# Norm weights folded into the weight conversion, row scaling on ScalarE, 48-row loads and a new order for the first 420 steps of a recurrent-attention and two-layer feed-forward kernel

## The chip, the cores and the metric

The kernel runs on one core of a Trainium2 chip. The metric is the device time of one execution in microseconds (us); it was 443.83 us before (median of 3 runs, 443.22 to 448.07).

## The reference

The input is a gated linear attention over 2 batches, 8 heads, 768 positions and head size 40, followed by two feed-forward layers on the 1536 rows of 320 features that it gives.

```
attention, for every t:  m_new = max(f + m, i)
    C = exp(f+m-m_new) * C + exp(i-m_new) * v k^T      n likewise with k
    y = sigmoid(o_gate) * (C q) / max(|n q|, 1)
layer 1:  rms = sqrt(mean(x*x) + 1e-06);  xn = x / rms * rms_g
    out1 = (silu(xn @ w_gate) * (xn @ w_val)) @ w_out      320 -> 1536 -> 320
layer 2:  h = out1 @ w_in;  max(0.01*h, h) @ w_out         320 -> 2048 -> 320
```

The weights and the output are float64 and float32 in memory: the kernel converts each weight tile from 64-bit numbers itself. `rms_g` has one number for each of the 320 features.

## The kernel before, in words

The 768 positions are cut into 6 chunks of 128, so there are 12 attention tiles T (chunk T // 2 of batch T % 2). In the early part of the program each tile passes through the same steps, and four kinds of work are interleaved by hand:

- **Gates.** DVE runs the scans over the gate rows (`sf`, `sa`), PE turns the rows into columns (`co`), ACT takes exponentials. For tiles 0 and 1, PE builds the argument of the exponential itself (`fa`, `rows_a`, from the split rows `A_hl` that `ah` writes); later tiles read it back from memory (`Ab`).
- **Attention of a tile.** PE: scores `qk` (`s`, L343). ACT: four exponentials per half (`arg`, L359). DVE: scores times exponentials (`p`, L390). PE: times the values (`av`, L403), the state of earlier chunks (`inn`, L413) and the new state (`kv`, L425). DVE: output gate `y1` (L458), reciprocal, `yr` (L472). ACT: sum of squares `sq` (L478).
- **The norm.** `y2` in three parts: DVE makes mean + epsilon from the sum (L485), POOL raises it to -1/2 (`pow`, L487), DVE refines that with one Newton step of three instructions (L489 to L491). Then `xn` (L496, DVE) multiplies the 128 x 320 rows by that column and by `gb`, the norm weights spread over all partitions; `xc` (ACT) copies 64 columns, `tp` (L507, PE) transposes, `xh` (ACT) and `xl` (L515, DVE) split the result into a high and a low part of `X`.
- **Weight conversion.** Each tile of A (512 columns), R (256) and B (320) weights goes through a shift on DVE (L548), a Prelu on ACT (L550), a shift-or on DVE (L552), a rounded copy on ACT (L573, L616, L627) and the remainder on DVE (L575, L619, L630).

The first feed-forward products, `U` (L658), need `X` of three tiles: `U.0.*` those of tiles 0 to 2, `U.1.*` those of tiles 3 to 5. `D` (L730) multiplies by the B weights. Each engine takes its instructions strictly in the order of the list `ORDER`, whose tokens name a step and its indices; there is no other scheduler. The token `id.1` is a product of ones (L229, `busy`) whose result nobody reads. The queue SP issues all transfers, in the same order list; q and k come by `ld_qk` (two halves of 40 rows of 4 KB, into one of three buffers), and `e` rows by `ld_e` (two halves of 40 rows of 2 KB).

Of the kernel before, what the change touches and what calls it, by code (L numbers as in the profile page):

```python
# [18 lines left out]
L = 128  # L19
# [36 lines left out]
wR.2 r.2 mask.3.1 rec.0 wA.1 a.1 rec.1 r.2 dq.2 a.1 yr.0 id.1 mask.3.0 arg.3.0 r.2 id.1 r.2 qk.2 th.1 st.0 y1.1 de.2
dA.2.6 eq.2 ux.1.2 co.1.1.2 cv.1.1.2 cv.0.2.6 sq.0 y2.0.0 yr.1 wA.2 kv.1 dgb p.2.0 av.2.0 arg.2.1 y2.0.1 p.2.1 y2.0.2
k.2 sq.1 y2.1.0 a.2 y2.1.1 a.1 xn.0 a.2 arg.3.1 a.1 dq.3 qk.3 p.3.1 dq.4 cb.0 wB.1 a.2 xc.0 b.1 dsl y2.1.2 th.2 a.2
dr.2.6 da.4 mask.4.1 wA.4 xn.1 av.2.1 inn.2 y1.2 xc.1 id.1 st.1 abs.2 id.1 id.1 id.1 p.3.0 rec.2 tp.0 id.1 b.1 tp.1
dn.3 yr.2 dr.1.2 mask.4.0 dc.1.2 a.4 sq.2 b.1 y2.2.0 kv.2 xh.1 wR.3 th.3 de.3 dE.2.6 k.3 b.1 id.1 xh.0 xl.0 av.3.0  # L60
co.1.2.6 cv.1.2.6 xl.1 cb.1 y2.2.1 y2.2.2 r.3 qk.4 eq.3 av.3.1 inn.3 dv.1.2 xn.2 arg.4.0 xc.2 tp.2 abs.3 r.3 r.3 c.3
rec.3 dn.5 kv.3 a.4 xh.2 arg.4.1 xl.2 U.0.1.1 p.4.0 k.5 y1.3 da.5 a.4 st.3 U.0.1.0 cb.3 p.4.1 th.5 T.0.1 dn.4 th.4
mask.5.0 wA.3 yr.3 sq.3 a.4 E.0.1 mask.5.1 a.3 arg.5.1 dc.2.6 de.4 r.3 arg.5.0 y2.3.0 a.3 eq.4 M.0.1 av.4.0 av.4.1
inn.4 dq.5 qk.5 y2.3.1 y1.4 p.5.1 U.0.0.0 p.5.0 T.0.0 E.0.0 dv.2.6 U.0.0.1 M.0.0 da.6 mask.6.1 arg.6.1 de.5 wB.0 abs.4
dq.6 a.3 rec.4 mask.6.0 av.5.0 av.5.1 S.0.1 eq.5 y2.3.2 yr.4 S.0.0 inn.5 kv.5 abs.5 b.0 xn.3 rec.5 b.0 sq.4 y2.4.0
# [103 lines left out]
def body(ctx: ExitStack, tc, ig, fg, qk, nat, wgv, wgr, wo1, wi2, wi2r, wo2, rg, cst, cst2, out):  # L169
# [940 lines left out]
```

## Time and profile before

| | |
|---|---|
| median of 3 runs | 443.83 us (443.22 to 448.07) |
| profiled execution, its own time | 444.82 us |
| span of the profiled execution | 443.0 us |
| PE busy | 429.1 us, 97% |
| DVE busy | 367.9 us, 83% |
| ACT busy | 280.7 us, 63% |
| POOL busy | 104.5 us, 24% |
| chain that ended last | PE 83%, DVE 8%, ACT 4%, DMA 2%, issue 2% |

PE is TensorE's product unit, DVE VectorE, ACT ScalarE, POOL GpSimd, SP the queue that issues transfers. Busy shares over the whole span hide that the program has stages: the first 80 us hold the attention of eight tiles and the conversion of the first weights, and the rest is nearly all feed-forward. So the profile is read by stretches, and for each stretch one asks what PE waited for and at which clock it ran.

### The profile page before, as it was taken

The numbers are of one execution on the slowest core, as the hardware profiler recorded it, in microseconds if no ns is written. First come the engines' busy times: TensorE is split into PE (matmuls) and PEld (weight loads), VectorE is DVE, ScalarE is ACT, GpSimd is POOL, SyncE is SP. The second block draws the span as 40 slices with busy tenths as digits, with TensorE's granted clock in tenths as the row PEclk, the third lists the DMA queues.
The fourth block names the chain that finished last, engine by engine and source line by source line (L and its number), as shares of the span: only waits on it lengthen the run. The fifth ranks groups of instructions, "written<-read, shape, count | busy, mean of one in ns | idle before, by whom it ended". The sixth has DMA issues, their size and how long they took to land.

```text
span 443.0 us, 9728 instructions
## 1 busy us (share of the span) xinstructions
PE 429.1 (97%) x3702; PEld 409.6 (92%) x3704; DVE 367.9 (83%) x827; ACT 280.7 (63%) x708; POOL 104.5 (24%) x166
## 2 busy tenths in 40 slices
PE   8897989999999999999999999999999999999997
PEld 4775978999999989999999999999999999999996
DVE  7998999677787758969989999888679897988775
ACT  5777866674664377644565565987866676577442
POOL 4644462431212000463736210010101010110000
PEclk9559999999999999999999999999999999999999
DMA  7987593653602124121200000004012311101005
GB/s 220 320 304 248 181 323 115 222 169 115 223 2 78 56 77 123 57 84 39 85 2 2 1 0 1 1 9 148 30 34 74 108 48 32 30 31 31 0 2 178
DMA packets 16119, 42.14 MB, mean 95 GB/s; under 512 B 2056, under 2 KB 4040, under 8 KB 16072
## 3 DMA queue, kind: packets, MB, share of 16 engines
q1 hardware_dynamic: 16072, 41.52, 28.4%
q8 instruction: 29, 0.48, 0.4%
q14 instruction: 18, 0.15, 0.1%
HBM read 39.45 MB, written 2.06 MB: 94 GB/s over the span
## 4 chain that ended last, share of the span: by engine, by line
PE 83%; DVE 8%; ACT 4%; DMA 2%; issue 2%; SPq 0%; DVEq 0%; ACTq 0%
PE h L808 13%; PE xa L730 10%; PE v L658 8%; PE g L658 8%; PE oa L981 6%; PE oa L979 6%; PE oa L980 6%; PE u L808 6%; PE xw L748 5%; PE h L814 3%; PE h L813 3%; PE s L343 2%; PE o L403 2%; PE u L813 1%; DMA Ab<-A_d 1%
## 5 line engine op out<-in xcount | busy, mean ns | idle before, releaser
L981 PE MATMUL oa<-wB,xl 128*128 128x320 f32 x192 | 59.3, 309 | 0.0
L980 PE MATMUL oa<-wB,xh 128*128 128x320 f32 x192 | 59.3, 309 | 0.0
L979 PE MATMUL oa<-wB,xh 128*128 128x320 f32 x192 | 59.3, 309 | 0.0
L658 PE MATMUL g<-X,wA 128*128 128x384 f32 x256 | 50.3, 341 | 1.8 <-DVE th L690 0.9
L991 DVE TENSOR_TENSOR x<-oa,x 128x320 f32<-128x320 f32 x84 | 39.5, 484 | 14.6 <-PE oa L981 13.9
L658 PE MATMUL v<-X,wA 128*128 128x384 f32 x256 | 49.9, 339 | 0.9 <-ACT X L511 0.7
L658 PEld LDWEIGHTS g<-X,wA 128*128 128x128 f32 x256 | 44.2, 188 | 3.9 <-DVE th L690 1.2
L658 PEld LDWEIGHTS v<-X,wA 128*128 128x128 f32 x256 | 44.5, 188 | 1.5 <-ACT X L511 0.8
L730 PE MATMUL xa<-sh,wB 128*128 128x384 f32 x160 | 45.9, 337 | 0.0
L590 POOL TENSOR_TENSOR sums<-w_A 128x128 f32<-128x128 f32 x8 | 3.9, 487 | 151.6 <-DVE w_A L552 147.0
L981 PEld LDWEIGHTS oa<-wB,xl 128*128 128x128 f32 x192 | 36.1, 188 | 0.1
L980 PEld LDWEIGHTS oa<-wB,xh 128*128 128x128 f32 x192 | 36.0, 188 | 0.0
L979 PEld LDWEIGHTS oa<-wB,xh 128*128 128x128 f32 x192 | 36.0, 188 | 0.0
L808 PE MATMUL h<-X,wA 128*128 128x384 f32 x144 | 32.2, 338 | 0.0
L730 PE MATMUL xa<-sl,wB 128*128 128x384 f32 x96 | 32.2, 336 | 0.0
L955 ACT ACTIVATE c<-c 128x384 f32<-128x384 f32 x48 | 25.2, 524 | 7.2 <-DVE c L852 3.4
L730 PEld LDWEIGHTS xa<-sh,wB 128*128 128x128 f32 x160 | 29.4, 188 | 0.1
L965 DVE TENSOR_TENSOR xl<-c,xh 128x384 fp32r<-128x384 f32 x48 | 26.0, 556 | 1.0 <-ACT xh L960 0.8
L960 ACT CAST xh<-c 128x384 fp32r<-128x384 f32 x48 | 24.3, 513 | 2.9 <-PE oa L980 2.2
L359 ACT ACTIVATE w<-Ab,aeu 128x128 f32<-128x128 f32 x80 | 25.3, 392 | 0.6 <-POOL Ab L363 0.6
L808 PEld LDWEIGHTS h<-X,wA 128*128 128x128 f32 x144 | 25.0, 188 | 0.1
L487 POOL TENSOR_TENSOR sm<-sm,mhalf 128x1 f32<-128x1 f32 x12 | 7.9, 661 | 66.5 <-DVE sm L485 66.5
(204 smaller groups left out, 1124.8 us busy)
## 6 DMA issues: line engine op xcount, KB each, us to landing
raw_B<-wo SPq DMA_DIRECT2D x28, 320.0 KB
raw_A<-wgv SPq DMA_DIRECT2D x12, 512.0 KB
nat<-nat SPq DMA_DIRECT2D x12, 484.0 KB
Ab<-A_d SPq DMA_DIRECT2D x10, 512.0 KB
raw_A<-wi SPq DMA_DIRECT2D x8, 512.0 KB
qkt<-qk SPq DMA_DIRECT2D x24, 160.0 KB
out<-x SPq DMA_DIRECT2D x12, 160.0 KB
eb<-e_d SPq DMA_DIRECT2D x20, 80.0 KB
```

The lines of the kernel that those rows point to most:

```text
L359: A.activation(w[:, j], src, AF.Exp, scale=-1.0, bias=col)
L658: PE.matmul(dst, a, x, start=(i == 0), stop=(i == len(seq) - 1))
L730: PE.matmul(xa, w, x, start=(k == 0), stop=(k == len(seq) - 1))
L748: PE.matmul(xas["w", g, i], a, x, start=(f == NE and k == 0), stop=(f == NF - 1 and k == len(seq) - 1),)
L808: PE.matmul(dst, x, y, start=first and j == 0, stop=j == 2, skip_group_check=not first)
L955: A.activation(t, src, AF.Prelu, alpha=0.01)
L960: A.copy(v["h"], v["t"])
L965: V.tensor_tensor(v["l"], v["t"], v["h"].bitcast(F32), op=ALU.subtract)
L979: PE.matmul(oa, v["h"][:, ts], wb[:, 0:DM], start=m == 0, stop=False)
L980: PE.matmul(oa, v["h"][:, ts], wb[:, DM:], start=False, stop=False)
L981: PE.matmul(oa, v["l"][:, ts], wb[:, 0:DM], start=False, stop=m == 1)
L991: V.tensor_tensor(dst, oas[k, p, i], dst, op=ALU.add)
```

## The change

It has five parts.

1. The norm weights are loaded as three columns `gcol` (128 x 3) in place of `gb` (128 x 320 by broadcast), and multiplied into the A and R weights of layer 1 when these are converted. ACT's copy of 512 columns becomes two scaled copies of 256, and DVE's remainder two instructions of 256 with a multiplication and a subtraction.
2. `xn`, now a scaling of the rows by one column alone, goes from DVE to ACT.
3. Epsilon is a 321st column of `y`, set once; the square on ACT carries the scale, so the sum comes out as the mean, and DVE's `y2.T.0` (L485) goes. The Newton step takes two instructions instead of three (the sign sits in the reciprocal's factor).
4. q, k and `e` are loaded as 48 rows per half instead of 40; the added rows are not used by the products.
5. The first 420 of some 1,930 tokens of the order are new. After `K.0.0.1`, `U.1.2.1` begins a tail that is the same as before but for the `y2.T.0` tokens. The number of `id.1` is 24 in both.

```diff
-id.1 id.1 id.1 id.1 z.0 z.1 z.2 did cr id.1 id.1 dfg dig id.1 id.1 id.1 wR.1 dq.0 ms id.1 sf.0.1 sa.0.1 ah sf.1.2 id.1
+ms id.1 z.4 id.1 dig cl z.5 z.0 z.2 z.1 dfg sf.0.1 sa.0.1 sf.1.2 sa.1.2 ev.1.2 did cr co.0.1.2 cv.0.1.2 uv.0.1 ah.0
...
-        for r in (slice(0, D), slice(64, 64 + D)):
+        for r in (slice(0, 48), slice(64, 112)):
             Q.dma_start(out=qkt[r].rearrange("p a j t -> p (a j t)"), in_=qk[T, r])
...
-            Q.dma_start(out=eb[64 * e:64 * e + D].rearrange("p j l -> p (j l)"), in_=e_v[b, c, e].partition_broadcast(D))
+            Q.dma_start(out=eb[64 * e:64 * e + 48].rearrange("p j l -> p (j l)"), in_=e_v[b, c, e].partition_broadcast(48))
...
-        A.activation(junk, t["yf"], AF.Square, accum_out=t["sm"][:, 8:9])
+        A.activation(junk, t["yx"], AF.Square, scale=2.0 * DM ** -0.5, accum_out=t["sm"][:, 8:9])
...
-        if i == 0:
-            V.tensor_scalar(out=v_, in0=ss, scalar1=1.0 / DM, scalar2=1e-6, op0=ALU.mult, op1=ALU.add)
-        elif i == 1:
+        if i == 1:
             G.tensor_tensor(z, v_, mhalf, op=ALU.pow)
         else:
             V.tensor_scalar(out=z2, in0=z, scalar1=z, scalar2=v_, op0=ALU.mult, op1=ALU.mult)
-            V.tensor_scalar(out=z2, in0=z2, scalar1=-0.5, scalar2=1.5, op0=ALU.mult, op1=ALU.add)
-            V.tensor_tensor(z, z, z2, op=ALU.mult)
+            V.tensor_scalar(out=zn, in0=z2, scalar1=3.0, scalar2=z, op0=ALU.subtract, op1=ALU.mult)
...
-        V.scalar_tensor_tensor(out=xn[:, 0:DM], in0=t["yf"], scalar=t["z"], in1=gb, op0=ALU.mult, op1=ALU.mult)
+        A.activation(xn[:, 0:DM], t["yf"], AF.Copy, scale=t["z"])
...
-        A.copy(w[:, 0:2], x)
+        for k in range(2):
+            A.activation(w[:, k], x[:, k], AF.Copy, scale=gcol[:, k:k + 1])
         yield
-        V.tensor_tensor(w[:, 2:4], x, w[:, 0:2].bitcast(F32), op=ALU.subtract)
+        for k in range(2):
+            V.scalar_tensor_tensor(
+                out=w[:, 2 + k], in0=x[:, k], scalar=gcol[:, k:k + 1], in1=w[:, k].bitcast(F32), op0=ALU.mult, op1=ALU.subtract,
+            )
```

What the new order moves is seen in the engines' own lists. First PE's list at the start of the program, before, from the ninth product of ones to the first scores (`pt` are columns, `A` the arguments of `fa`, `s0` the scores of tile 0):

```order
L229 MATMUL busy_138<-const-bfloat16-1.0 128x512
L229 MATMUL busy_150<-const-bfloat16-1.0 128x512
L229 MATMUL busy_159<-const-bfloat16-1.0 128x512
L251 MATMUL pt0_0_165<-consts_87,x2_92 128x16
L261 MATMUL A0_0_178<-consts_r_88 128x512
L264 MATMUL A0_0_178<-A_hl_89,consts_r_88 128x128 x4
L261 MATMUL A1_1_191<-consts_r_88 128x512
L264 MATMUL A1_1_191<-A_hl_89,consts_r_88 128x128 x4
L261 MATMUL A0_1_203<-consts_r_88 128x512
L264 MATMUL A0_1_203<-A_hl_89,consts_r_88 128x128 x4
```

And the same place now, from PE's first product:

```order
L230 MATMUL busy_127<-const-bfloat16-1.0 128x512
L230 MATMUL busy_130<-const-bfloat16-1.0 128x512
L252 MATMUL pt0_1_153<-consts_87,x2_92 128x16
L252 MATMUL pt0_0_167<-consts_87,x2_92 128x16
L262 MATMUL A1_0_175<-consts_r_88 128x512
L265 MATMUL A1_0_175<-A_hl_89,consts_r_88 128x128 x4
L262 MATMUL A1_1_198<-consts_r_88 128x512
L265 MATMUL A1_1_198<-A_hl_89,consts_r_88 128x128 x4
L252 MATMUL pt1_0_204<-consts_87,x2_92 128x16
L262 MATMUL A0_0_218<-consts_r_88 128x512
```

Eleven products of ones at the front became two, and the arguments of tile 1 come ahead of those of tile 0.

Second, PE's list around the state product of tile 2 (`o1_2` from `Cbd0`), before:

```order
L403 MATMUL o1_2_494<-nat2_238,w2_1_511 32x41 x16
L413 MATMUL o1_2_494<-Cbd0_98,eb2_105 32x82 x16
L229 MATMUL busy_615<-const-bfloat16-1.0 128x512
L229 MATMUL busy_620<-const-bfloat16-1.0 128x512
L229 MATMUL busy_622<-const-bfloat16-1.0 128x512
L229 MATMUL busy_624<-const-bfloat16-1.0 128x512
L507 MATMUL tp0_629<-consts_87,xn0_531 128x128 x3
```

And now, from the last of tile 1's state products to the state product of tile 2:

```order
L426 MATMUL o1_1_383<-nat1_172,Kt1_110 40x41
L230 MATMUL busy_538<-const-bfloat16-1.0 128x512
L230 MATMUL busy_545<-const-bfloat16-1.0 128x512
L230 MATMUL busy_547<-const-bfloat16-1.0 128x512
L230 MATMUL busy_569<-const-bfloat16-1.0 128x512
L230 MATMUL busy_571<-const-bfloat16-1.0 128x512
L252 MATMUL pt1_1_573<-consts_87,x2_92 128x16
L230 MATMUL busy_579<-const-bfloat16-1.0 128x512
L230 MATMUL busy_581<-const-bfloat16-1.0 128x512
L414 MATMUL o1_2_450<-Cbd0_98,eb2_105 32x82 x16
```

Seven products of ones now stand right ahead of that state product (three more follow it), where four followed it before.

Third, DVE's list from the remainder of the B weights of tile 2's time to `X` of tile 2 (`sm2` are the norm's columns of tile 2, `X` from `tp0`, `tp1`, `tp2` the split of tiles 0, 1, 2), before:

```order
L631 TENSOR_TENSOR wB_1_654<-w32_B1_561,wB_1_654 128x64
L515 TENSOR_TENSOR X_93<-tp0_629,X_93 128x3x128
L255 COPY aeu_94<-pt1_2_698 128x64
L515 TENSOR_TENSOR X_93<-tp1_636,X_93 128x3x128
L489 TENSOR_SCALAR sm2_618<-sm2_618 128x1
L490 TENSOR_SCALAR sm2_618<-sm2_618 128x1
L491 TENSOR_TENSOR sm2_618<-sm2_618 128x1
L548 TENSOR_SCALAR w32_R3_711<-raw_R3_667 128x256
L305 COPY gdec_95<-pg1_647 128x8
L496 SCALAR_TENSOR_TENSOR xn2_758<-y2_612,sm2_618,gb_91 128x320
```

And now:

```order
L578 SCALAR_TENSOR_TENSOR wA_2_475<-w32_A2_492,gcol_91,wA_2_475 128x256 x2
L489 TENSOR_SCALAR sm2_599<-sm2_599 128x1
L490 TENSOR_SCALAR sm2_599<-sm2_599 128x1
L306 COPY gdec_95<-pg1_682 128x8
L553 SCALAR_TENSOR_TENSOR w32_A4_694<-raw_A4_684,w32_A4_694 128x512
L514 TENSOR_TENSOR X_93<-tp0_671,X_93 128x3x128
L256 COPY aeu_94<-pt0_2_713 128x64
L460 SCALAR_TENSOR_TENSOR y0_106<-nat3_543,o1_3_618 128x320
L514 TENSOR_TENSOR X_93<-tp1_707,X_93 128x3x128
L514 TENSOR_TENSOR X_93<-tp2_760,X_93 128x3x128
```

The norm's columns of tile 2 have moved ahead of `X` of tiles 0 and 1, `xn2` has left DVE's list, and the three `X` splits stand close together.

## Rows read from the trace of the kernel before

**Rows 1.** Busy time by stretch: us; PE, PEld, DVE, ACT, POOL (instructions), granted clock, DMA share, GB/s

```profile
0.00:10.65 10.65, 8.62 (x32) 4.25 (x32) 8.32 (x21) 5.94 (x17) 5.04 (x18) 1.00 0.76 221
10.65:34.50 23.85, 21.26 (x337) 16.45 (x337) 22.29 (x55) 16.99 (x51) 12.69 (x18) 0.51 0.91 312
34.50:44.02 9.52, 7.06 (x163) 5.44 (x163) 7.75 (x27) 7.43 (x25) 4.45 (x8) 0.98 0.68 239
44.02:80.25 36.23, 33.84 (x606) 31.01 (x608) 33.38 (x81) 25.44 (x78) 18.31 (x27) 1.00 0.64 213
80.25:443.00 362.75, 358.35 (x2567) 352.50 (x2566) 296.15 (x646) 224.89 (x540) 64.02 (x98) 1.00 0.19 62
```

**Rows 2.** PE's waits, 0 to 80.25: us in total, times, longest

```profile
PE tp L507 <- DVE X L515: 1.3, 1, 1.3
...
PE g L658 <- DVE th L690: 0.9, 1, 0.9
```

**Rows 3.** Timeline of PE: start us, us, engine, line, operation, names, shape, count, idle before

```profile
10.45 0.50 PE L261 MATMUL A<-consts_r 128*128 128x512 f32 x1
...
11.73 4.08 PE L343 MATMUL s<-qkt 40*128 40x128 f32 x31
...
28.36 2.49 PE L343 MATMUL s<-qkt 40*128 40x128 f32 x16
...
31.33 1.32 PE L413 MATMUL o<-Cbd,eb 104*32 104x82 f32 x32
32.98 1.49 PE L229 MATMUL busy<-const-bfloat16-1.0 128*128 128x512 bf16 x3 [0.33 <-issue]
...
80.25 2.95 PE L658 MATMUL v<-X,wA 128*128 128x384 f32 x16
```

**Rows 4.** Timeline of DVE

```profile
5.03 0.28 DVE L270 TENSOR_TENSOR A_hl<-x,A_hl 16x128 fp32r<-16x128 f32 x1
...
6.17 0.47 DVE L241 TENSOR_TENSOR_SCAN x<-x 16x128 f32<-16x128 f32 x1
...
16.33 2.48 DVE L390 TENSOR_TENSOR w<-s,w 128x512 f32<-128x512 f32 x4
...
34.31 0.47 DVE L458 SCALAR_TENSOR_TENSOR y<-nat,o 128x320 f32<-128x320 f32 x1
...
40.02 0.27 DVE L489 TENSOR_SCALAR sm<-sm 128x1 f32<-128x1 f32 x1
...
62.87 2.00 DVE L496 SCALAR_TENSOR_TENSOR xn<-y,sm,gb 128x320 f32<-128x320 f32 x1
```

**Rows 5.** Timeline of POOL

```profile
37.63 0.55 POOL L487 TENSOR_TENSOR sm<-sm,mhalf 128x1 f32<-128x1 f32 x1 [1.95 <-DVE sm L485]
...
63.24 1.28 POOL L367 TENSOR_TENSOR eb<-eb,qkt 104x512 f32<-104x512 f32 x1
```

**Rows 6.** Groups of PE by form, 10.65 to 34.50: count | busy us, mean ns | idle before

```profile
L403 PE MATMUL o<-nat,w 128*32 128x41 f32 x192 | 4.2, 272 | 2.2 <-DVE w L390 1.7 <-PE o L425 0.5
...
L425 PE MATMUL o<-nat,Kt 128*64 128x41 f32 x16 | 2.2, 311 | 0.0
```

**Rows 7.** Groups of DVE by form, 0 to 80.25

```profile
L496 DVE SCALAR_TENSOR_TENSOR xn<-y,sm,gb 128x320 f32<-128x320 f32 x6 | 4.7, 783 | 0.0
...
L575 DVE TENSOR_TENSOR wA<-w_A,wA 128x512 fp32r<-128x512 f32 x5 | 3.9, 772 | 0.0
...
L485 DVE TENSOR_SCALAR sm<-sm 128x1 f32<-128x1 f32 x6 | 0.9, 148 | 0.3 <-ACT junk L478 0.3
```

**Rows 8.** Groups of ACT by form, 0 to 80.25

```profile
L359 ACT ACTIVATE w<-A,aeu 128x128 f32<-128x128 f32 x16 | 4.3, 362 | 0.5 <-DVE aeu L255 0.5
...
L447 ACT ACTIVATE nat<-nat 128x320 f32<-128x320 f32 x8 | 3.7, 464 | 0.3 <-DMA nat<-nat 0.3
...
L573 ACT CAST wA<-w_A 128x512 fp32r<-128x512 f32 x5 | 3.0, 605 | 0.0
```

**Rows 9.** A stretch in which SP issues only loads of q and k (columns of rows 1)

```profile
50.00:51.00 1.00, 1.00 (x8) 1.00 (x7) 1.00 (x4) 1.00 (x4) 1.00 (x3) 1.00 0.65 246
```

More of the change, by code (lines that the diff above doesn't have):

```diff
@@ L56 @@
[L56 to L65, printed above, removed]
@@ L193, in body @@
     consts_r = attc.tile([128, 272], F32R, name="consts_r")
-    A_hl = attc.tile([48, L], F32R, name="A_hl")
+    A_hl = attc.tile([48, 2, L], F32R, name="A_hl")
     ident, mask = consts[:, 0:128], consts[:, 128:256]
@@ L198, in body @@
     blk = sel[:, 128:136]
-    gb = attc.tile([128, DM], F32, name="gb")
+    gcol = const.tile([128, 3], F32, name="gcol")
     x2 = const.tile([128, NTILE, 3, L], F32, name="x2")
@@ L207, in body @@
     QK = [attc.tile([128, 2, 4, L], F32, name=f"qkt{n}") for n in range(3)]
-    EB = [attc.tile([104, 4, L], F32, name=f"eb{n}") for n in range(3)]
+    EB = [attc.tile([128, 4, L], F32, name=f"eb{n}") for n in range(3)]
+    Y = [attc.tile([128, DM + 1], F32, name=f"y{n}") for n in range(3)]
     Kt = [attc.tile([128, 4, 104], F32, name=f"Kt{b}") for b in range(2)]
@@ L456, in att_y1 @@
         num = t["num"]
-        t["y"] = y = work.tile([128, H, D], F32, tag="y", name=f"y{T}")
+        t["yx"] = Y[T % 3]
+        t["y"] = y = Y[T % 3][:, 0:DM].rearrange("p (h d) -> p h d", h=H)
         V.scalar_tensor_tensor(
@@ L465, in att_rec @@
         r = t["sm"][:, 0:8]
-        V.tensor_scalar(out=r, in0=r, scalar1=1.0, scalar2=2.0, op0=ALU.max, op1=ALU.mult)
+        V.tensor_scalar(out=r, in0=r, scalar1=1.0, scalar2=-2.0, op0=ALU.max, op1=ALU.mult)
         V.reciprocal(r, r)
@@ L476, in att_sq @@
         t = st_[T]
-        junk = work.tile([128, DM], F32, tag="junk", name=f"junk{T}", bufs=1)
-        A.activation(junk, t["yf"], AF.Square, accum_out=t["sm"][:, 8:9])
+        junk = work.tile([128, DM + 1], F32, tag="junk", name=f"junk{T}", bufs=1)
+        A.activation(junk, t["yx"], AF.Square, scale=2.0 * DM ** -0.5, accum_out=t["sm"][:, 8:9])
     def att_y2(T, i):
         t = st_[T]
-        ss, v_, z, z2 = (t["sm"][:, i:i + 1] for i in range(8, 12))
-        t["z"] = z
-        if i == 0:
-            V.tensor_scalar(out=v_, in0=ss, scalar1=1.0 / DM, scalar2=1e-6, op0=ALU.mult, op1=ALU.add)
-        elif i == 1:
+        v_, z, z2, zn = (t["sm"][:, i:i + 1] for i in range(8, 12))
+        t["z"] = zn
+        if i == 1:
             G.tensor_tensor(z, v_, mhalf, op=ALU.pow)
@@ L518, in memsets @@
         G.memset(mhalf, -0.5)
+        for y in Y:
+            G.memset(y[:, DM:], (DM * 1e-6) ** 0.5)
         G.memset(A_hl.bitcast(F32), 0.0)
@@ L614, in weight_r @@
         halves = [(up_weights(2 * i + e), slice(64 * e, 64 * e + 64), slice(64 - 64 * e, 128 - 64 * e)) for e in range(2)]
+        first = i < NF // 2
         for w, hi, lo in halves:
-            A.copy(w[hi, 4], x[hi])
+            if first:
+                A.activation(w[hi, 4], x[hi], AF.Copy, scale=gcol[hi, 2:3])
+            else:
+                A.copy(w[hi, 4], x[hi])
         yield
         for w, hi, lo in halves:
-            V.tensor_tensor(w[lo, 4], x[hi], w[hi, 4].bitcast(F32), op=ALU.subtract)
+            if first:
+                V.scalar_tensor_tensor(
+                    out=w[lo, 4], in0=x[hi], scalar=gcol[hi, 2:3], in1=w[hi, 4].bitcast(F32), op0=ALU.mult, op1=ALU.subtract,
+                )
+            else:
+                V.tensor_tensor(w[lo, 4], x[hi], w[hi, 4].bitcast(F32), op=ALU.subtract)
         yield
```

232 lines of the change are left out of this document (121 added, 111 removed).

## The prediction, made before the result was known

> **What bounds the kernel now.** I read the busy time by stretch first [rows 1]. The reader is to see two programs in one. From 80.25 us on, PE is busy 358.35 of 362.75 us at a granted clock of 1.00, while DVE has 296.15 and ACT 224.89. From `U.1.2.1`, the product that starts there [rows 3], the order is the old one. So a gain or loss at that start reaches the end one for one, and the question is when 80.25 comes. Ahead of it PE is idle 2.03 us up to 10.65, 2.59 up to 34.50, 2.46 up to 44.02 and 2.39 up to 80.25, together 9.5. The second stretch stands out: at a clock of 0.51, the level of 1.2 GHz, PE's work there costs about twice what it costs at 2.4 GHz, DVE is busy 22.29 of 23.85 us, and the DMA share is 0.91.
>
> Then I read PE's waits [rows 2]: the two long ones are 1.3 us of `tp` for DVE's `X` and 0.9 of `g` for `th`. Last the timelines [rows 3 to 5], for the chain that makes the first `U` possible: scores, `p`, values, state product, `y1`, norm, `xn`, `tp`, `X`. I cut it into three terms: T1 up to `y1` of tile 2 (34.31 [rows 4]), T2 from there to `U.0.1` (44.02 [rows 1]), T3 from there to `U.1.2.1`. A gain is counted positive.
>
> **T1, the start.** PE's work is the same; only places differ. Before, `A_hl` is written by 5.31 and a second pair of scans follows until 6.64 [rows 4]. In the new order that pair (1.33 us) and some six small operations of about 0.15 each (the L485 row [rows 7]) stand ahead of `ah`: `A_hl` comes at about 7.5. With two products of ones at the front I let PE run at half clock from there. Four arguments follow, each 1.28 us (from 10.45 to 11.73 [rows 3]), until about 12.7; scores of tile 0, half of the 4.08 us that two tiles took, to 14.7. ACT's exponentials cost 4.3/16 = 0.27 us [rows 8], four of them 1.1, partly under the scores: first `p` at about 15.2, against 16.33 [rows 4], and the values of tile 0 from about 15.9.
>
> From there PE's list at half clock: values 4.2/3 = 1.4 us a tile [rows 6], scores 2.04, state 1.1 (2.2 for two [rows 6]), a product of ones 0.5 (1.49 for three [rows 3]). Up to the scores of tile 3 it is 1.4 + 2.04 + 0.5 + 2.04 + 0.7 + 0.5 + 1.1 + 0.7 + 0.5 + 0.7 = 10.2, so these start at 26.1; before it was 28.36. Scores, two products of ones, values and state (2.04 + 1.0 + 0.7 + 1.1) lead to 30.9. Then stand the seven products of ones and the state product of tile 2, which took 1.32 [rows 3]: its end lies at 33.3 at the earliest (0.23 each, half the price above, and 0.8) and 35.7 at the latest, against 32.65. DVE has to wait about 2 us for the scores of tile 1 at half clock (14.7 + 1.4 + 0.5 + 2.04 = 18.6, with its own work done by 16.6), and by the 16 us of work that its list then holds it comes to `y1` of tile 2 at about 35.0, where before it was 34.31. So T1 = **-0.7**, from +1.0 (the state product ends at 33.3 and DVE is free) to -2.7 (the dearest products, and DVE behind them by 1.3).
>
> The loads grow by a fifth (48 rows for 40) in a stretch whose DMA share is 0.91. While only such loads were in flight the share was 0.65 [rows 9], that is some 10 of the 16 engines. No row shows 48 rows. The bounds: nothing, if the rows spread over engines now idle, or a fifth of a transfer on the path, within T1's lower end; I take nothing. The Trainium skill, page "DMA: Bandwidth & Descriptors", section "Why a DMA increments its semaphore by 16 and not by 1", says that the outer size decides how many engines share a transfer, the largest divisor up to 16: 10 for 40 rows, which the 0.65 bears out, and 16 for 48. By it each engine would move 3 rows for 4, and the term would be slightly above nothing.
>
> **T2, norm and first U.** Between `y1` of tile 2 and `U.0.1` lie 9.7 us. POOL's power ended at 38.18 [rows 5], but DVE came to the Newton step at 40.02 [rows 4], since the `X` splits of tiles 0 and 1 stood ahead and waited: 1.84 us. These stand behind it now. L485 (0.15 and 0.3 of idle [rows 7]) goes, and one Newton instruction of the same kind with its hop, 0.2. That is 2.5 us at most on the norm. `xn` moves from DVE (a mean of 0.78 with its stalls [rows 7]) to ACT; the nearest row is 0.46 [rows 8]: nothing gained or lost, and ACT, busy 7.43 of 9.52 [rows 1], has room. If another ACT instruction stood ahead, the cost is up to 0.6 (the copy of 512 [rows 8]). What is late next: `X` of tiles 0 and 1, which now stand behind, and PE's own 7.06 us of work in this stretch. I take **+2.4**, from 0.8 (the splits become the last wait) to 3.4 (with all of the 0.9 us by which PE's idle time of 2.46 could shrink beyond my sum).
>
> **T3, up to U.1.2.1.** The 1.3 us stall of `tp` [rows 2] followed an `xn` that took 2.00 us, from 62.87 to 64.87, while POOL's product ran from 63.24 to 64.52 [rows 4, 5]. With `xn` on ACT this goes. The 0.9 for `th` stays. DVE, busy 33.38 of 36.23 us [rows 1], loses 4.7 us of `xn` in the first 80 us and 0.9 of L485 [rows 7]; the remainder in two pieces of 256 columns costs about the same 0.77 plus one more start of some 0.15 for each of five tiles. ACT's two scaled copies for one of 0.605 [rows 8] are bounded by 0.6 and 1.2, five times 0.3 on average, and six `xn` at 0.46 add 2.8: with 25.44 of 36.23 us ACT covers it. If that cover were gone the exponentials would be late by up to 0.6. I take **+1.2**, from -0.8 (a caught remainder takes xn's place) to 2.4 (all of PE's idle time).
>
> A rule of the Trainium skill, page "SBUF — State Buffer", section "Who interferes with whom", speaks against the change. A DVE instruction with two inputs in SBUF and a GpSimd instruction that reads SBUF exclude each other, and the first holds the other up for its whole length. The 2.00 us beside POOL's 1.28 agrees. By it each split remainder can be caught twice where it could be caught once, up to 1.28 us each time, and T3 would be -0.8 where the row of `xn` alone gives 1.2.
>
> **The sum** is -0.7 + 2.4 + 1.2 = 2.9 us. The profiled execution took 444.82, so 441.9 for it; it lay 0.99 above the median of 443.83, and the same gain from the median gives **440.9**. The ends: -2.7 + 0.8 - 0.8 = -2.7, or 446.5; and 1.0 + 3.4 + 2.4 = 6.8, or 437.0.
>
> **The rivals.** *Full gain.* All terms at their upper ends: the first scores come early enough that the norm is ready whenever PE is. For it: 9.5 us of PE's time are idle, and the order is free to fill it. Against it: DVE at 93% in two stretches. 437.0; chance 0.30.
>
> *The clock stays low (slower).* Before, the clock was 1.00 up to 10.65, fell after the products of ones at the front, and came back at 34.50, behind three of them in a row [rows 1, 3]. With two at the front it may never be 1.00 early, and if the ten around the state product of tile 2 are broken by waits for DVE, it stays at 0.5 until the `U` products. Then T1 is -2.5, and PE's work between that state product and `U.0.1`, about 7.7 us (7.06 in the stretch and what precedes 34.50 of it), takes 15.4 where 11.4 us lay before: -4.0. With T3 of 1.2 the loss is 5.3, or 449.1. It decides once more than about 40% of that work runs at half clock. Against it: ten such products nearly together are more than the three that were enough. Chance 0.08.
>
> *The change does not do what it says.* The second inputs on DVE stay (remainders, splits), POOL catches them as before, and the wider loads lengthen a DMA stage at 0.91. T1 -2.5, T2 1.0, T3 0: -1.5, or 445.3. For it: DVE's list gets shorter by only 36 of 829 instructions. Against it: the waits that go have names and places. Chance 0.17.
>
> The forecast itself, with a range of 439.4 to 443, has 0.45.
>
> **How the numbers follow.** About 1%, 4.4 us, is what a measurement of this kernel can tell from no change: 439.4 and 448.3. Faster by more takes the full gain, 0.30; slower by more takes the low clock, 0.08; the forecast and the third rival lie between, 0.62. The range leaves out the low clock and about half of the third rival on one side and the last part of the full gain on the other, some 0.2: 436.5 to 444.5.
>
> **What the next profile would show.** T1 is right if `y1` of tile 2 starts near 35 and the clock is 1.00 from about 34; wrong if the first `p` comes after 17. T2 is right if the Newton step starts within 0.3 us of POOL's end and `U.0.1` stands near 42.3; wrong if `X` of tile 0 or 1 ends the wait there. T3 is right if no wait of `tp` for `X` over 1 us is left and `U.1.2.1` starts near 77.3. The whole is wrong if the stretch behind `U.1.2.1` no longer takes 362.75 us, for instance because ACT's new work or a caught remainder stalls PE there.

## The result, and the profile after

The changed kernel took 450.65 us in the median of 10 runs (449.22 to 453.38), against 443.98 before. The ratio is 1.0126, with a 95% interval of 1.0098 to 1.0154: it is slower. Forecast were 440.9 us and a range of 436.5 to 444.5.

The profiled execution took 449.22 us, 4.40 more than that of before, so it shows two thirds of the loss of the medians (it is the fastest of the ten). First the busy time by stretch of the changed kernel (columns as in [rows 1]), cut where the three terms of the prediction end:

```profile
0.00:10.65 10.65, 5.88 (x17) 3.38 (x17) 8.58 (x26) 5.01 (x12) 4.60 (x19) 1.00 0.78 253
10.65:24.30 13.65, 12.01 (x170) 10.13 (x171) 8.60 (x19) 10.59 (x34) 5.22 (x9) 1.00 1.02 267
24.30:31.00 6.70, 3.62 (x120) 2.66 (x117) 5.73 (x16) 5.31 (x16) 3.93 (x7) 1.00 0.93 323
31.00:46.11 15.11, 13.72 (x230) 8.83 (x232) 10.71 (x33) 11.03 (x34) 8.24 (x14) 0.89 0.80 242
46.11:82.86 36.75, 34.22 (x605) 31.19 (x606) 30.48 (x77) 30.42 (x92) 17.16 (x26) 1.00 0.79 230
82.86:447.40 364.54, 358.87 (x2570) 352.61 (x2566) 293.76 (x635) 228.18 (x548) 64.79 (x98) 1.00 0.20 62
```

`U.1.2.1` starts at 82.86, where it was 80.25 [rows 3], and the stretch behind it takes 364.54, where it was 362.75 [rows 1]. So 2.61 us are lost ahead of it and 1.79 behind. DVE is no longer full: 8.60 of 13.65 us from 10.65 to 24.30, and 30.48 of 36.75 in the second stage, where it was 33.38 of 36.23. ACT has 30.42 there, where it had 25.44 [rows 1].

PE's timeline after (columns as in [rows 3]), the places of the prediction's first two terms:

```profile
13.12 2.17 PE L344 MATMUL s<-qkt 40*128 40x128 f32 x16
...
26.94 1.27 PE L344 MATMUL s<-qkt 40*128 40x128 f32 x16
...
31.61 1.04 PE L426 MATMUL o<-nat,Kt 128*64 128x41 f32 x16 [2.43 <-ACT Cbd L443]
32.59 2.31 PE L230 MATMUL busy<-const-bfloat16-1.0 128*128 128x512 bf16 x5
...
35.53 0.78 PE L414 MATMUL o<-Cbd,eb 104*32 104x82 f32 x32
...
37.78 0.66 PE L426 MATMUL o<-nat,Kt 128*64 128x41 f32 x16
...
45.52 0.44 PE L672 MATMUL g<-X,wA 128*128 128x384 f32 x1
46.11 1.49 PE L672 MATMUL g<-X,wA 128*128 128x384 f32 x7 [0.15 <-DVE X L514]
```

The same 16 scores take 2.17 us at 13.12 and 1.27 at 26.94, so PE ran at the level of 1.2 GHz until about 24 us, although the clock column stands at 1.00 there: the price tells it. Then PE waits 2.43 us for the state product of tile 1, and five products of ones behind it cost 0.46 each, the price of the low level again (the clock of that stretch is 0.89).

DVE's timeline after:

```profile
6.45 0.28 DVE L271 TENSOR_TENSOR A_hl<-x,A_hl 16x128 fp32r<-16x128 f32 x1
...
15.72 1.29 DVE L391 TENSOR_TENSOR w<-s,w 128x512 f32<-128x512 f32 x2 [1.62 <-ACT w L360]
18.46 0.49 DVE L460 SCALAR_TENSOR_TENSOR y<-nat,o 128x320 f32<-128x320 f32 x1 [1.45 <-ACT nat L448]
...
31.00 0.47 DVE L460 SCALAR_TENSOR_TENSOR y<-nat,o 128x320 f32<-128x320 f32 x1
...
38.59 0.49 DVE L460 SCALAR_TENSOR_TENSOR y<-nat,o 128x320 f32<-128x320 f32 x1 [0.92 <-PE o L426]
...
41.91 0.27 DVE L489 TENSOR_SCALAR sm<-sm 128x1 f32<-128x1 f32 x1 [0.45 <-POOL sm L487]
```

The three L460 rows are `y1` of tiles 0, 1 and 2. That of tile 2 starts at 38.59, where it was 34.31 [rows 4]; the Newton step follows POOL's end at once:

```profile
40.90 0.97 POOL L487 TENSOR_TENSOR sm<-sm,mhalf 128x1 f32<-128x1 f32 x1 [2.70 <-ACT junk L480]
```

In the second stage the 1.3 us of `tp` [rows 2] are gone, and PE waits elsewhere (columns as in [rows 2]):

```profile
PE v L672 <- issue: 1.3, 1, 1.3
...
PE o L426 <- ACT sm L453: 1.1, 1, 1.1
```

Behind `U.1.2.1` three waits make most of the 1.79 us. PE's timeline after, and then before:

```profile
167.97 3.06 PE L672 MATMUL g<-X,wA 128*128 128x384 f32 x16 [1.07 <-ACT th L697]
...
174.10 2.69 PE L672 MATMUL g<-X,wA 128*128 128x384 f32 x14 [0.30 <-issue]
177.50 0.62 PE L672 MATMUL g<-X,wA 128*128 128x384 f32 x2 [0.71 <-DVE wA L629]
```

```profile
164.30 3.04 PE L658 MATMUL g<-X,wA 128*128 128x384 f32 x16 [0.40 <-ACT th L683]
...
173.10 0.62 PE L658 MATMUL g<-X,wA 128*128 128x384 f32 x2 [0.39 <-DVE wA L619]
```

The waits grow from 0.79 to 2.08. What they wait for stands behind weight conversions. ACT's timeline ahead of the first of them, after and then before:

```profile
165.09 1.03 ACT L623 ACTIVATE wA<-w_R,gcol 64x256 fp32r<-64x256 f32 x2 [0.73 <-DVE w_R L553]
166.13 1.28 ACT L697 ACT_TABLE_LOAD   x1
167.43 0.49 ACT L697 ACTIVATE th<-g 128x384 f32<-128x384 f32 x1
```

```profile
161.62 0.82 ACT L616 CAST wA<-w_R 64x256 fp32r<-64x256 f32 x2 [0.81 <-DVE w_R L552]
```

The load of 1.28 us stands in both. Of the 0.67 by which this wait grew, 0.21 is the scaled R copy itself; the rest is its later start, behind DVE's shift-or. The A conversions are dearer too, by form over the whole span, after and then before:

```profile
L575 ACT ACTIVATE wA<-w_A,gcol 128x256 fp32r<-128x256 f32 x24 | 10.9, 502 | 3.4 <-DVE w_A L553 3.3
L578 DVE SCALAR_TENSOR_TENSOR wA<-w_A,gcol,wA 128x256 fp32r<-128x256 f32 x24 | 10.5, 481 | 0.0
```

```profile
L575 DVE TENSOR_TENSOR wA<-w_A,wA 128x512 fp32r<-128x512 f32 x12 | 8.7, 723 | 0.1
...
L573 ACT CAST wA<-w_A 128x512 fp32r<-128x512 f32 x12 | 7.4, 615 | 2.2 <-DVE w_A L552 2.1
```

Half the columns cost far more than half: 502 ns for 256 against 615 for 512 on ACT.

### The profile page after: what moved, and what is told of

It reads as the page before. It is cut to its first block, busy times and chain, and to the rows that moved or that the text cites. A ratio compares the mean times of both kernels' runs of the same rounds, so it can differ in the third digit from the quotient of the medians.

```text
span 447.4 us, 9734 instructions
## 1 busy us (share of the span) xinstructions
PE 428.3 (96%) x3700; PEld 408.8 (91%) x3704; DVE 357.9 (80%) x803; ACT 290.5 (65%) x732; POOL 103.9 (23%) x169
## 3 DMA queue, kind: packets, MB, share of 16 engines
q1 hardware_dynamic: 16688, 42.47, 30.9%
## 4 chain that ended last, share of the span: by engine, by line
PE 86%; DVE 6%; DMA 3%; ACT 2%; issue 2%; POOL 1%; SPq 0%; DVEq 0%; POOLq 0%; ACTq 0%
PE h L822 13%; PE xa L744 10%; PE v L672 9%; PE g L672 8%; PE oa L995 6%; PE oa L994 6%; PE oa L993 6%; PE u L822 6%; PE xw L762 5%; PE h L828 3%; PE h L827 2%; PE s L344 2%; DMA Ab<-A_d 1%; PE o L404 1%; PE u L827 1%
## 5 line engine op out<-in xcount | busy, mean ns | idle before, releaser
L979 DVE TENSOR_TENSOR xl<-c,xh 128x384 fp32r<-128x384 f32 x48 | 26.1, 556 | 1.0 <-ACT xh L974 0.8
L720 ACT CAST sh<-th 128x384 fp32r<-128x384 f32 x32 | 16.2, 512 | 13.5 <-DVE th L711 11.9
```

Of the source, the lines that this page charges most:

```text
L979: V.tensor_tensor(v["l"], v["t"], v["h"].bitcast(F32), op=ALU.subtract)
```

## The experiments

The ratio is to runs of the kernel before beside each edit. The start of `U.1.2.1` and the stretch behind it are of the one profiled execution.

| run | edit | median us | ratio [95%] | `U.1.2.1` | behind |
|---|---|---|---|---|---|
| before | | 443.98 | 1 | 80.25 | 362.8 |
| changed | | 450.65 | 1.0126 [1.0098, 1.0154] | 82.86 | 364.5 |
| 1 | changed, 40 rows | 451.28 | 1.0130 [1.0098, 1.0161] | 85.08 | 364.5 |
| 2 | before, 48 rows | 445.28 | 1.0002 [0.9969, 1.0036] | 80.55 | 362.8 |
| 3 | changed, old order | 450.06 | 1.0109 [1.0044, 1.0173] | 81.17 | 364.4 |
| 4 | changed, `y1.1` early | 450.86 | 1.0123 [1.0070, 1.0175] | 86.77 | 364.6 |
| 5 | changed, 8 more ones in front | 454.37 | 1.0203 [1.0149, 1.0257] | 89.19 | 364.7 |
| 6 | before, part 1 alone | 447.51 | 1.0035 [1.0005, 1.0066] | 81.84 | 364.2 |
| 7 | before, part 2 alone | 443.70 | 0.9957 [0.9929, 0.9985] | 79.75 | 363.2 |
| 8 | changed, no folding | 449.73 | 1.0089 [1.0053, 1.0125] | 84.09 | 363.1 |
| 9 | changed, old order, 40 rows | 446.44 | 1.0035 [1.0009, 1.0062] | 82.32 | 364.5 |
| 10 | before, part 3 alone | 443.90 | 0.9986 [0.9959, 1.0012] | 79.62 | 362.8 |
| 11 | before, new order alone | 462.13 | 1.0373 [1.0333, 1.0414] | 95.04 | 362.9 |
| 12 | changed, 7 ones dropped | 451.31 | 1.0125 [1.0078, 1.0172] | 86.66 | 364.6 |
| 13 | old order, then new, 40 rows | 451.38 | 1.0121 [1.0076, 1.0166] | 83.63 | 364.6 |
| 14 | new order, then old, 40 rows | 451.17 | 1.0115 [1.0072, 1.0158] | 83.66 | 364.6 |
| 15 | changed, ones in two gaps | 450.79 | 1.0102 [1.0082, 1.0122] | 84.40 | 364.6 |
| 16 | before, `xn` on ACT, POOL weighs | 445.59 | 0.9999 [0.9969, 1.0029] | 80.94 | 363.8 |
| 17 | 4, and `y1.2` early | 453.35 | 1.0209 [1.0159, 1.0259] | 88.35 | 364.6 |
| 18 | 17, and two moves | 454.97 | 1.0231 [1.0159, 1.0302] | 87.76 | 364.6 |

### The loads: 1 and 2

Run 1 takes the wider loads back in the changed kernel, run 2 puts them alone into the kernel before.

```diff
-        for r in (slice(0, 48), slice(64, 112)):
+        for r in (slice(0, D), slice(64, 64 + D)):
```

> The changed kernel with q, k and e loaded as 40 rows per half again, all else as changed. Theory of the loads (48 rows make the packets of all loads slower: in the changed kernel a 4096-byte packet took 0.249 us in the median between 10.65 and 24.3 us, before 0.159): about 447 us, 3 to 4 below the changed kernel's 450.65, and the DMA share of 10 to 25 us falls from 1.02 to about 0.9. Theory of the order (the output y1 of tile 1 stands too late on DVE's list, and the state product of tile 1 waits 2.4 us for it): no more than 1 us below 450.65. Theory of the new work on ACT: the same, no more than 1 us.

> The kernel before with 48 rows per half of q, k and e and nothing else changed; the added rows are not used by the products. Theory of the loads: 2 to 4 us slower than before (446 to 448). Theory of the order and theory of ACT: within 1 us of 443.98.

Neither moved the time beyond its interval (some 1.5 to 2 us), so on these two orders the loads are not the cause. The share moved, though (run 1, to be held against the row of the same stretch above):

```profile
10.65:24.30 13.65, 12.00 (x170) 10.12 (x170) 8.64 (x19) 10.47 (x34) 5.19 (x9) 1.00 0.87 289
```

### The order on the same code: 3, 9 and 11

Runs 3 and 9 are the changed code with the list of before, without its `y2.T.0`, the columns' load `dgb` put behind `wR.1`; run 9 also has 40 rows. Run 11 is the kernel before with the new list.

```diff
 # run 11: before, ORDER alone
-id.1 id.1 id.1 id.1 z.0 z.1 z.2 did cr id.1 id.1 dfg dig id.1 id.1 id.1 wR.1 dq.0 ms id.1
+ms id.1 z.4 id.1 dig cl z.5 z.0 z.2 z.1 dfg sf.0.1 sa.0.1 sf.1.2 sa.1.2 ev.1.2 did cr
...
-L.0.1 sq.3 y2.3.1 r.3
+L.0.1 sq.3 y2.3.0 y2.3.1 r.3
```

> The changed code with the order of before (without the y2.T.0 steps, and with the load of the three norm-weight columns put behind wR.1 at the front, since the conversions need them now). Theory of the order: 441 to 444, since parts 1 to 3 of the change take work from DVE. Theory of the loads: 446 to 448, as much as the loads cost alone. Theory of ACT's new work: 447 to 451, since the scaled copies and xn stay.

> The changed code with the order of before (as in the third experiment) and 40 rows per half again: parts 1 to 3 alone. Theory that the parts add up (folding +1.5 us, xn on ACT -2.0, loads nothing, as measured apart): 444.5 to 446. Theory that the wider loads matter once the other parts are there: 444.5 to 446 here as well, where the third experiment had 450.06. Theory that parts 1 to 3 hurt together on any order, since each moves DVE and ACT by tenths of a us and the granted clock falls in other places: 448 to 451.

> The kernel before with the new order alone (its code and its 40 rows as before, the y2.T.0 steps put ahead of the POOL steps). Theory that the new order is the main loss (state product of tile 1 late, clock low until 24.5 us and again later): 448.5 to 451, U.1.2.1 at 83 or later. Theory that the new order is good only with parts 1 to 3 or is itself a gain: 440 to 446.

With 40 rows the old order gives 1.0035 and the new one 1.0130 (run 1): the new order costs 0.95%, or 4.2 us, on the same code. With 48 rows, which the changed kernel has, it is 1.0109 [1.0044, 1.0173] against 1.0126, and no cost of the order is shown. Run 3 had four runs from 447.45 to 453.74, so whether the wider loads cost something there stays open. On the code of before the new order costs 3.7%, but that is not its price here: the list was made for `xn` on ACT, and in run 11 PE's `tp` waits 4.9 us for `xn` on DVE.

### The parts alone: 6, 7, 10 and 8

Run 6 is before with part 1: the conversions of the changed kernel, and `xn` on DVE by the rows' column alone.

```diff
-        A.copy(w[:, 0:2], x)
+        for k in range(2):
+            A.activation(w[:, k], x[:, k], AF.Copy, scale=gcol[:, k:k + 1])
...
-        V.scalar_tensor_tensor(out=xn[:, 0:DM], in0=t["yf"], scalar=t["z"], in1=gb, op0=ALU.mult, op1=ALU.mult)
+        V.tensor_scalar(out=xn[:, 0:DM], in0=t["yf"], scalar1=t["z"], scalar2=None, op0=ALU.mult)
```

> The kernel before with part 1 alone: norm weights as three columns in the conversion of the A and R weights, xn on DVE by the row's column alone, the load of the columns at the front, the rest and the order as before. Theory of the conversion: the stretch behind U.1.2.1 takes 1.7 us more than 362.75 by two waits of g, as in the changed kernel, and the whole is 446 to 449. Theory that xn on ACT is what costs: 444, with a stretch of 362.75.

Run 7 is before with `xn` on ACT:

```diff
-        V.scalar_tensor_tensor(out=xn[:, 0:DM], in0=t["yf"], scalar=t["z"], in1=gb, op0=ALU.mult, op1=ALU.mult)
+        A.activation(xn[:, 0:DM], t["yf"], AF.Copy, scale=t["z"])
```

> The kernel before with part 2 alone: xn on ACT; the norm weights are left out of the computation. Theory of the conversion: 442 to 444.5, stretch behind U.1.2.1 of 362.75. Theory that xn on ACT is what costs (it waits in ACT's list behind conversions): 446 to 449.

Run 10 is before with part 3. It has two `y` buffers by turns, so the rows of tile 7 are replaced by those of tile 9 ahead of their norm; the amount of work is the same.

```diff
-            V.tensor_scalar(out=z2, in0=z2, scalar1=-0.5, scalar2=1.5, op0=ALU.mult, op1=ALU.add)
-            V.tensor_tensor(z, z, z2, op=ALU.mult)
+            V.tensor_scalar(out=zn, in0=z2, scalar1=3.0, scalar2=z, op0=ALU.subtract, op1=ALU.mult)
```

> The kernel before with part 3 alone: epsilon as a column, the scale on the square, two Newton instructions; two y buffers as before. Theory that the parts add up and this one is small: 443.5 to 446. Theory that part 3 is what the sum of the others lacks: 448 to 450.

Run 8 takes the folding out of the changed kernel:

```diff
-        for k in range(2):
-            A.activation(w[:, k], x[:, k], AF.Copy, scale=gcol[:, k:k + 1])
+        A.copy(w[:, 0:2], x)
```

> The changed kernel with the conversion of A and R as before, so that the norm weights are left out of the computation; xn on ACT, 48 rows and the new order stay. Theory of the conversion: the stretch behind U.1.2.1 returns to about 362.8 and the whole is 2 us or more below 450.65, near 447 to 448.5. Theory of the order's start (late y1, low clock): the head stays, so not below 447. Theory that xn on ACT is what costs: within 0.7 us of 450.65.

Folding costs 0.35% (1.6 us) by run 6 and 0.37% by run 8 against the changed kernel, `xn` on ACT gains 0.43% (1.9), part 3 nothing that can be told from no change. In run 6 `xn` on DVE also lost its second input, so its 0.35% is what is left after any gain from that. The stretch behind `U.1.2.1` is the clearest: 364.2 to 364.7 in every kernel that folds, 362.8 to 363.8 in every other. In run 6 the three waits of the changed kernel are there (1.07, 0.30 and 0.73), and PE's timeline of run 8 has the old ones back:

```profile
168.53 3.04 PE L659 MATMUL g<-X,wA 128*128 128x384 f32 x16 [0.39 <-ACT th L684]
...
177.33 0.63 PE L659 MATMUL g<-X,wA 128*128 128x384 f32 x2 [0.37 <-DVE wA L620]
```

### Where y1 stands: 4, 17 and 18

```diff
 # run 4
-av.2.0 wA.1 ex.2.6 ux.1.2 abs.1 rec.1 r.1 a.1
+av.2.0 wA.1 ex.2.6 ux.1.2 abs.1 y1.1 rec.1 r.1 a.1
...
-qk.3 p.3.0 y1.1 id.1
+qk.3 p.3.0 id.1
 # run 17, besides
-id.1 inn.2 abs.2 a.2
+id.1 inn.2 abs.2 y1.2 rec.2 yr.2 sq.2 a.2
 # run 18, besides
-yr.3 r.3 yr.4 S.0.1 U.0.0.0 T.0.0 E.0.0
+yr.3 S.0.1 U.0.0.0 T.0.0 E.0.0 r.3 yr.4
-kv.5 st.4 st.5 da.6 mask.6.0 qk.6
+st.4 da.6 mask.6.0 qk.6 kv.5 st.5
```

> The changed kernel with one step of the order moved: y1 of tile 1 directly behind abs of tile 1, ahead of the conversions on DVE. Theory of the order: the state product of tile 1 starts at about 29.2 us and no longer at 31.6, and the whole is 1.5 to 2.5 us below 450.65. Theory of the loads: less than 1 us, as the next wait is for a load.

PE's timeline of run 4:

```profile
27.46 2.08 PE L343 MATMUL s<-qkt 40*128 40x128 f32 x16
...
31.14 1.08 PE L425 MATMUL o<-nat,Kt 128*64 128x41 f32 x16
32.15 2.31 PE L229 MATMUL busy<-const-bfloat16-1.0 128*128 128x512 bf16 x5
...
35.25 0.78 PE L413 MATMUL o<-Cbd,eb 104*32 104x82 f32 x32
```

The wait of 2.43 us is gone, so it was for `y1` of tile 1, which reads the bank that the state product writes, and not for the copy on ACT that the changed kernel's row names: in run 4 the state product at 31.14 ran ahead of that copy (ACT's timeline of run 4):

```profile
32.36 0.33 ACT L442 COPY Cbd<-C 40x164 f32<-40x164 f32 x1
```

But the state product of tile 2 came only 0.28 us earlier: here the scores at 27.46 take 2.08, since the clock stayed at the low level some ten us longer. The whole did not move (1.0123). Later the clock fell again (run 4):

```profile
50.00:58.00 8.00, 6.02 (x141) 5.53 (x138) 7.74 (x23) 7.54 (x22) 3.27 (x5) 1.00 0.96 267
58.00:69.00 11.00, 10.18 (x116) 9.18 (x115) 6.52 (x19) 6.49 (x23) 2.88 (x5) 0.53 0.38 131
```

> The changed kernel with y1 of tile 1 directly behind abs of tile 1, and y1, rec, yr and the square of tile 2 directly behind abs of tile 2, ahead of the state product of tile 2. Theory of the place on DVE's list: y1 of tile 2 at about 36.4 in place of 38.6, U.0.1 1.5 to 2.5 us earlier, the whole 448 to 449.5. Theory of other limits (the X split of the three tiles and the weights come no earlier, or the clock falls elsewhere): 450 to 452.

> As the run before, and besides the state product of tile 5 behind the scores of tile 6, and E of U.0.0 ahead of a conversion step and of yr of tile 4. Theory that the waits of PE near 57 and 61 us are what the second stage loses: 1 to 3 us below the run before, 446 to 448. Theory that DVE and ACT bound that stage by their sum: within 1 us of the run before.

In run 17 `y1` of tile 2 came 1.68 us earlier, and yet the first product of `U.0.1` 2.00 us later (47.52, in the changed kernel 45.52). The moved steps held others up: PE waited 0.75 us for `y1` ahead of the new state of tile 2, then 1.26 for `p` of tile 3, and the clock fell once more (three products of ones took 1.49):

```profile
36.91 0.49 DVE L459 SCALAR_TENSOR_TENSOR y<-nat,o 128x320 f32<-128x320 f32 x1 [0.67 <-ACT sm L452]
```

```profile
37.54 0.63 PE L425 MATMUL o<-nat,Kt 128*64 128x41 f32 x16 [0.75 <-DVE y L459]
39.44 0.78 PE L403 MATMUL o<-nat,w 128*32 128x41 f32 x32 [1.26 <-DVE w L390]
...
40.84 1.49 PE L229 MATMUL busy<-const-bfloat16-1.0 128*128 128x512 bf16 x3
...
47.52 2.08 PE L671 MATMUL g<-X,wA 128*128 128x384 f32 x8
```

Runs 17 and 18 are slower than the changed kernel, and 18 is no faster than 17. An earlier `y1` brought no time back in any of the three. What it is worth with the clock and the other steps unmoved was not shown.

### The products of ones: 5, 12 and 15

```diff
 # run 5
-ms id.1 z.4 id.1 dig cl
+ms id.1 z.4 id.1 id.8 dig cl
 # run 12: the seven id.1 between kv.1 and inn.2 go
-kv.1 id.1 st.1 cb.1 dn.3 id.1 id.1 yr.1 ... xn.0 id.1 id.1 co.1.1.2 cv.1.1.2 xn.1 xc.1 id.1 id.1 inn.2
+kv.1 st.1 cb.1 dn.3 yr.1 ... xn.0 co.1.1.2 cv.1.1.2 xn.1 xc.1 inn.2
 # run 15
-mask.7.0 arg.7.0 U.0.2.0
+mask.7.0 arg.7.0 id.3 U.0.2.0
-b.0 b.3 kv.5
+b.0 b.3 id.3 kv.5
```

> The changed kernel with eight more products of ones at the front, where PE waits 3.4 us for the first scans. Theory of the clock (the changed kernel lost the products of ones at the front, so the arguments and the first scores run at the 1.2 GHz level, and later gaps let the clock fall in some executions): the granted clock rises near 4.5 us and no longer near 24.5, the four arguments take half as long (0.9 us less each), the first p starts about 2.5 us earlier than at 15.7, and the whole is 1.5 to 3 us below 450.65. Theory of DVE's and ACT's lists (conversions stand ahead, the clock plays no part): within 0.5 us of 450.65.

> The changed kernel without the seven products of ones ahead of the state product of tile 2, which took 3.0 us there. Theory that they lie on the path to y1 of tile 2: 2 to 3 us below 450.65, y1 of tile 2 at 36 in place of 38.6. Theory of the clock: they are what brings the clock back at 34.8, so without them the clock stays low to U and the whole is 1 to 4 us above 450.65.

> The changed kernel with three products of ones ahead of U.0.2.0 and three ahead of the state product of tile 5, where PE waits 1.3 to 2.0 and 0.8 to 1.7 us. Theory of the clock in the second stage: it no longer falls between 58 and 69 us, the runs lie close together near 449, 1 to 2 us below 450.65. Theory that the gaps cost only their own length: 450.65 to 451.5, as ones fill time that is lost anyhow.

PE's timeline of run 5:

```profile
6.89 0.63 PE L264 MATMUL A<-A_hl,consts_r 48*128 48x128 f32 x4 [1.02 <-DVE A_hl L270]
...
9.39 1.11 PE L264 MATMUL A<-A_hl,consts_r 48*128 48x128 f32 x4
...
13.46 0.79 PE L343 MATMUL s<-qkt 40*128 40x128 f32 x2 [1.19 <-DMA qkt<-qk]
14.63 2.07 PE L343 MATMUL s<-qkt 40*128 40x128 f32 x14 [0.38 <-DMA qkt<-qk]
```

The clock did rise: the first arguments take 0.63, but those at 9.39 take 1.11 again. What PE gained there it lost at once, waiting 1.57 us for the first q and k. The ratio went from 1.0126 to 1.0203, some 3.4 us. Run 12 shows no difference (1.0125), so no cost and no use of the seven products above its interval, some 2 us, is shown. In run 15 the clock stays up where it fell in run 4:

```profile
58.00:69.00 11.00, 10.22 (x138) 8.88 (x140) 10.13 (x28) 9.57 (x32) 3.75 (x7) 1.00 0.59 181
```

Its four runs lie within 0.9 us (450.56 to 451.42), where the ten of the changed kernel spread over 4.2, but the median is the same, and the ratio of 1.0102 lies within the two intervals.

### Which half of the order, and a third version: 13, 14 and 16

Run 13 plays the old list until both `U.0.1` products are issued and then what is left in the order of the new one; run 14 the other way round.

```diff
 # run 13: the old list up to de.4, then the new list without the tokens played
-... dc.2.6 de.4 r.3 arg.5.0 y2.3.1 a.3 eq.4 M.0.1
+... dc.2.6 de.4 (new list from here)
```

> The changed code with 40 rows, the old order up to and with both U.0.1 products, and from there the new order for what is left. Ends of the scale: 446.4 (all old) and 451.3 (all new). Theory of the start (late y1 of tiles 1 and 2, low clock at the front): 445.5 to 447.5. Theory of the second stage (gaps of 1 to 2 us near 57 and 61 us after which the clock falls): 449.5 to 452.

> The changed code with 40 rows, the new order up to and with both U.0.1 products, and from there the old order for what is left. Theory of the start: 449.5 to 452. Theory of the second stage: 445.5 to 447.5, and the clock does not fall after 50 us.

Both give the loss of the whole new order. So it does not lie in one half alone; a seam between two lists may cost something of its own, and this was not separated.

```diff
 # run 16: before, besides run 7's edit
             G.tensor_tensor(z, v_, mhalf, op=ALU.pow)
+            G.tensor_tensor(t["yf"], t["yf"], gb, op=ALU.mult)
```

> An attempt at a version better than both: the kernel before with xn on ACT, and the norm weights multiplied into the rows by POOL right behind its power, so that no weight conversion changes; the load of the norm weights is put earlier. Theory that xn on DVE cost 2 us and folding is what took it back: 443 to 444.5, 1 to 2 us below before. Theory that POOL's product (two operands beside DVE's, about 0.9 us on the norm's path for each tile) takes the gain back: 445 to 447.

The gain of run 7 is gone: POOL's product takes it back, and no version here that does the whole computation beats the kernel before.

## Why the prediction was wrong, point by point

**T1, from -0.7 to -4.3.** This step failed. Up to the scores of tile 3 it held: `A_hl` 6.73 (7.5 forecast), first `p` 15.72 (15.2), those scores 26.94 (26.1). Then the state product of tile 1 ended at 32.65, not 30.9, by the wait of 2.43; that of tile 2 at 36.31, not 33.3 to 35.7; and `y1` of tile 2 started at 38.59, not 35.0. I read two places of the order wrongly. DVE's list was summed as work (16 us) and not as a queue: `y1` of tile 1 stands behind conversions, and the state product waits for it (run 4). (Nor do 18.6 and 16 give 35.0, but 34.6.) And I took `y1` of tile 2 as waiting for the state product `inn` alone, where it now waits for the next state product on the same bank too (38.59, 0.92 for L426). Moving both `y1` (run 17) gave no time back: new waits of 0.75 and 1.26 took their place, and PE ran at the low clock for longer (until about 32, from 39.0 to 42.4 and from 62.9 to 69.7). So these waits explain the places in the trace; that they cause the loss of time is not shown.

**T2, forecast 2.4, measured 2.2.** Right, and for the reason given: 7.52 us from `y1` of tile 2 to `U.0.1` in place of 9.7, with the Newton step 0.04 us behind POOL's end at 41.87, where it was 1.84.

**T3, from +1.2 to -0.5.** The stall of `tp` went as forecast, and the 0.9 for `th` too, but the row L426 <- L453 and the 1.3 us ahead of `U.0.2.0` took their place. PE was idle for 2.53 us, where it was 2.39, so the term that failed is the gain in PE's waits. DVE's idle time rose from 2.85 to 6.27 us, so it was no longer the amount of its work that counted.

**Behind U.1.2.1, from 0 to -1.8.** The sum has no term for this stretch, as its order is the old one, though the conversions change there too; only the last sign names a stall. PE's 4.4 us of idle time left little to gain, but nothing forbade a loss. In T3 I had the price of two scaled copies for one about right (0.3 us more for each tile, measured 0.39) and called it covered by ACT's free time. ACT has 228.18 of 364.54 us there, and yet a `g` waits for a `th` that is queued behind such copies. Runs 6 and 8 show that folding alone does it.

The four together are -4.4 us, the 4.40 between the profiled executions, where the sum said +2.9. Of these 7.3 us, 3.6 lie in T1, 0.2 in T2, 1.7 in T3 and 1.8 in the stretch without a term.

**The low clock**, the rival on the other side with a chance of 0.08, described more than the forecast did. It had the clock low until the `U` products. In the profiled execution it was low until about 24 us and once more behind 31; in run 4 also from 58 to 69, where I had not looked. Its time of 449.1 lies near the 450.65, but that is luck, since its place was not the one I gave. Nor did the changed kernel spend longer at the low level. By the prices of the products ahead of the clock's first rise (the eleven at the front of before took 4.17 us) and the granted clock behind it, the kernel before was there until about 4 us and from 10.9 to 34.8, the changed one until about 24.5 and from 31.4 to 34.8. That is some 28 us each, in which PE was busy for 24.3 us before and 21.3 after. So in these two executions the low clock alone does not make the difference.

**The wider loads at nothing** were right on the order and code of before (1.0002) and on the new ones (1.0130 without, 1.0126 with); on the old order with the new code it stays open (1.0035 without, 1.0109 with).

**The third rival's count** was off: DVE's list got shorter by 24 instructions (827 to 803), not 36, since the twelve A remainders became two each.

**What stays open.** The new order costs 4.2 us by comparison of whole orders with 40 rows; with 48 the same comparison shows nothing. No single place of it was shown to be the cause: late `y1`, products of ones, the two later waits, and either half were tried. The parts apart on the old order sum to -0.9 us (1.6 - 1.9 - 0.6), together they are +1.5. The four intervals added up leave that difference near the noise, and runs 6 and 7 both drop `xn`'s second input on DVE, so a gain from that is counted twice in the sum. The clock may be part of both, since it rises and falls elsewhere after each edit, and it could not be held fixed.

## What to carry to other kernels

A stretch in which the critical engine is busy 99% can still lose: a covered cost needs its cover at that place in the queue, not in the stretch's sum. For a new order, follow the queue of each in-order engine instruction by instruction, with who waits behind it, and what else uses the same bank. Where the clock moves with every edit, compare several whole versions before a wait in one trace is called the cause.

## What the runs showed of the hardware

- **48 rows.** With the same order and code, 48 rows raised the DMA share from 10.65 to 24.30 us from 0.87 to 1.02, while 289 GB/s became 267. In the kernel before the same edit (run 2) raised the share there from 0.88 to 1.04 and the GB/s from 301 to 322, and the time stayed. So in both the share grew by more than the bytes moved. The Trainium skill, page "DMA: Bandwidth & Descriptors", section "Why a DMA increments its semaphore by 16 and not by 1", gives a rule by which 48 rows go to 16 engines; the rise of the share agrees, but that each would be done sooner, as I worked out from it, did not show.
- **The clock.** In the changed kernel PE was busy 12.01 of 13.65 us from 10.65 to 24.30, at the prices of 1.2 GHz throughout (scores 2.17 and 2.08). In run 5, behind ten products of ones, the arguments at 6.89 ran at the price of 2.4 GHz, and those at 9.39 at that of 1.2 GHz again, though PE's one long wait between was the 1.02 us ahead of 6.89.
- **Two inputs on DVE.** Moving `xn`, which has two inputs in SBUF, from DVE to ACT gained 1.9 us (run 7). The Trainium skill, page "SBUF — State Buffer", section "Who interferes with whom", has a DVE instruction with two SBUF inputs contend with a POOL instruction that reads SBUF. The trace of before agrees: `xn` there has a mean of 665 ns with one of 2.00 us beside POOL, and in run 6, with one input, 500. How much of the 1.9 us that is, and how much DVE's shorter list, was not separated. In the changed kernel the remainder of the conversion on DVE (L578) has such inputs too, but there the trace shows little of it: its mean of 481 ns is 0.05 us above the 0.43 of each in the pair of 0.87 at 33.98 us.
